# Weight groups narrowed in stages: one stage a step, with VectorE's background passes put ahead of the next step's own

## The chip, the cores and the metric

One core of one Trainium2 chip runs one program. The metric is device time in microseconds (us) for one execution; the kernel before takes 1035.78 us (median of 3 runs, 1034.14 to 1037.46). Engine names in the rows: PE is TensorE's matmul, PEld its weight load, DVE is VectorE, ACT is ScalarE, POOL is GpSimd, SP issues the DMAs.

## The reference, cut to what matters

```
X = np.fft.fft(np.fft.fft(x, axis=1), axis=2).real      # x: (2, 3008, 256)
t = X.reshape(6016, 256)
h = t @ w_in;  g = max(h, 0)**2;  t = g @ w_out          # w_in (256, 2048), w_out (2048, 256)
h = t @ w2_in; g = h / (1 + exp(-1.702 h)); return g @ w2_out
```

All values are float32. TensorE multiplies in the format `F32R`, so the kernel splits each operand into a high part (a cast to F32R) and a low part (the value less its high part) and sums three products: high times high, high times low, low times high.

## The kernel before, in words

The spectrum is folded by symmetry into 8 blocks of 378 or 376 columns, each in an even and an odd half. The first MLP is a list of 128 **steps**, `steps`; step i takes one block j and one slice f of 128 of the 2048 hidden features. In a step:

- TensorE runs `front1` (L442 to L456): six matmuls into a fresh PSUM tile `psa`, of which there are two. Front i+2 therefore waits until VectorE has read the tile of front i to its end.
- VectorE makes `p` (L710) and the two halves of `h` (L712, L713); the last of them frees the `psa` tile.
- ScalarE makes the squared ReLU (L719, L720) and the high part `gh` (L722). In twelve steps (the set `SV`) VectorE does the ReLU (L717) instead.
- GpSimd, or VectorE in the steps of `VSTEPS`, makes the low part `gl` (L76) of the step before.
- TensorE runs `back` (twelve matmuls, L468) for step i-4 (`LAG`), so an undisturbed step is 18 matmuls.

Where a run of steps on one block ends (after steps 3, 7, 15, 23, 35, 39, 47, 63, 79, 95, 111), `store` (L573 to L582) copies the two accumulators `psb` out four steps later, one on ScalarE, one on VectorE. The next block's `back` needs those PSUM tiles.

Beside the steps runs **background** work (L558), as generators: each item that a generator yields is one or a few instructions. The table `PLAN` gives each job a first step, a rate (items a step) and a step by which it must be done. From step 18 on (`THROTTLE`) a background instruction may not be issued ahead of the step's last `h` and `gh` (`issue_after`); otherwise a list scheduler orders each engine's queue, and VectorE's background passes may stand behind or in between the `p` and `h` of later steps. Every engine works its queue in the order in which it was written.

The job that the change touches most prepares a **group** of weights. The weights come as 64-bit words and are narrowed to float32 by `narrow` (L162 to L180): ScalarE takes an absolute value (L169), VectorE makes four passes (clamp L170, shift and mask L171, or-in of the sign L178, add L180), and the low word is scaled (L175 on ScalarE for the groups in `RA`, L177 on VectorE for the others). Then `widen` or `widen_in` makes high and low parts; for `widen_in` (the second MLP's first matrix) GpSimd makes four differences (L233) and the low parts `w2i` in two rounds, and for `widen` it makes the low part `w` in most groups. All groups of the second MLP go through one buffer `ue`, so ScalarE's and VectorE's first passes on a group wait until GpSimd has read the group before. The jobs are `conv` (six groups, steps 3 to 36), `w2a` (three groups, 55 to 78) and `w2b` (five groups, 85 to 117). Seven of the eight groups of `w2a` and `w2b` are not in `RA`.

`odd_k` (L398) makes the two odd blocks of a batch: `split_eo` casts them to a high and a low part `eo`, and `nyquist` has TensorE read both parts (L418, L419).

After the 128 steps the second MLP runs from a schedule written by hand; nothing of it is touched.

Of the kernel before, what the change touches and what calls it, by code (L numbers as in the profile page):

```python
# [13 lines left out]
ALU = mybir.AluOpType  # L14
# [49 lines left out]
def spectral_two_mlps_kernel(  # L64
# [7 lines left out]
    def f32(ap):  # L72
        return ap.bitcast(F32)
# [88 lines left out]
    def narrow(raw, ue, key=None):  # L162

        r = raw.rearrange("p (n w) -> p n w", w=2)
        lw, hw = r[:, :, 0], r[:, :, 1]
        u = ue[:, 0]
        uu, eu = u.bitcast(U32), ue[:, 1].bitcast(U32)

        yield lambda: A.activation(out=u, in_=f32(hw), func=AF.Abs)  # L169
        yield lambda: V.tensor_scalar(out=u, in0=u, scalar1=LEAST, scalar2=TOP, op0=ALU.max, op1=ALU.min)  # L170
        yield lambda: V.tensor_scalar(out=uu, in0=uu, scalar1=3, scalar2=0x3FFFFFF8,  # L171
                                      op0=ALU.logical_shift_left, op1=ALU.bitwise_and)

        if key in RA:
            yield lambda: A.activation(out=eu, in_=lw, func=AF.Copy, scale=2.0 ** -29)  # L175
        else:
            yield lambda: V.tensor_scalar(out=eu, in0=lw, scalar1=2.0 ** -29, scalar2=None, op0=ALU.mult)  # L177
        yield lambda: V.scalar_tensor_tensor(out=eu, in0=hw, scalar=0xC0000000, in1=eu,  # L178
                                             op0=ALU.bitwise_and, op1=ALU.bitwise_or)
        yield lambda: V.tensor_tensor(out=uu, in0=uu, in1=eu, op=ALU.add)  # L180
# [6 lines left out]
    def widen(mlp, kind, g, temps, dest, then=None, tag="xt"):  # L187
        low = G if LOW[mlp, kind, g] == "G" else V
        raw = raws.pop((mlp, kind, g))
        ue = temp(temps, tag)  # L190
        yield from narrow(raw, ue, (mlp, kind, g))
        if then:
            then()
        w = dest.tile([P, 2, 1024], F32R, tag="w", name="w")
        o = ue[:, 0]
        if (mlp, kind) == (0, 0):

            o = ue[:, 1]
            a, c = ue[:, 0, 0:512], ue[:, 0, 512:1024]
            yield lambda: (G if g in EOG else V).tensor_tensor(out=o[:, 0:512], in0=a, in1=c, op=ALU.add)  # L200
            yield lambda: V.scalar_tensor_tensor(out=o[:, 512:1024], in0=a, scalar=mask, in1=c,
                                                 op0=ALU.mult, op1=ALU.subtract)
        yield lambda: A.copy(w[:, 0], o)
        yield lambda: sub(low, w[:, 1], o, w[:, 0])
        if mlp and (kind, g) in PARKED:
            park((mlp, kind, g), w)
        weights[mlp, kind, g] = w

    parked = {}

# [187 lines left out]
    def odd_k(b, pool, tag="xt", later=0):  # L398

        wd = WID[2]  # L400
        w = temp(pool, tag).rearrange("p a b -> p (a b)")
        a = w[:, 0:wd]
        e2, e3 = (w[:, i * wd:(i + 2) * wd].rearrange("p (r k) -> p r k", r=2) for i in (1, 3))
        c0, c1 = cst[b, 2][:, :, 0:wd], cst[b, 3][:, :, 0:wd]

        def sums(par):
            pe = ps_a()
            z = (zc[b], zs[b])[par]
            halves(pe[:, 0, 0:wd], pe[:, 1, 0:wd],
                   [(z[:, :, 2 + par, 0:P], c0), (z[:, :, 3 - par, 0:P], c1)])  # L410
# [12 lines left out]

        yield lambda: sums(0)
        yield lambda: sums(1)
        yield lambda: split_eo(b, 2, e2)
        yield lambda: nyquist(2)
        while at_step[0] < later:
            yield lambda: None
        yield lambda: split_eo(b, 3, e3)  # L430
        yield lambda: nyquist(3)


# [94 lines left out]
    def at(name, job):  # L528
        i, rate, end = PLAN[name]
        plan.setdefault(i, []).append((name, rate, job))  # L530
        if end is not None:
# [3 lines left out]
    at("even01", lambda: even_k(0, 1, h_temps))  # L535
    at("odd0", lambda: odd_k(0, xp, "x2", 36))
    at("conv", lambda: chain(*(
        widen(0, k, g, xp, (winp, wq)[k], tag=("t", "x0")[k],
              then=(lambda k=k, g=g: load_w(0, k, g + 1)) if g < 3 else None)
        for g in (1, 2, 3) for k in range(2))))  # L540
    at("x3", lambda: iter([lambda: load_x(3)]))
    at("x4", lambda: iter([lambda: load_x(4)]))
# [99 lines left out]
    def w2_jobs(lo, hi):  # L642
        for i in range(lo, hi):
            k, g = order[i]
            dest = w2a if i < 6 else w2b
            then = (lambda i=i: load_w(1, *order[i + 2])) if i + 2 < 8 else (lambda: load_y(0)) if i == 6 else None
            if k == 0:
                yield from widen_in(g, temp(cv2), dest, then=then)
            else:
                yield from widen(1, 1, g, cv2, dest, then=then)  # L650

    def y_first():
        yB["odd"] = raw_tile(1, F32R).rearrange("p (a b) -> p a b", a=2)
# [26 lines left out]
        yield from y_job(j)  # L680

    held = []
    by_hand = ExitStack()
    for i in range(n):

        if i == PLAN["fold5"][2]:
# [17 lines left out]
        elif done:  # L704
# [2 lines left out]
        h = m.tile([P, 2, NP], F32, tag="h", name="h", bufs=4)  # L707
        hv = h[:, :, 0:wd]
        p = m.tile([P, NP], F32, tag="p", name="p")
        V.scalar_tensor_tensor(out=p[:, 0:wd], in0=e128[blocks[j]][:, 0:wd], scalar=w1n_t[:, 0, f:f + 1],  # L710
                               in1=ps[:, 0, 0:wd], op0=ALU.mult, op1=ALU.add)
        V.tensor_tensor(out=h[:, 0, 0:wd], in0=p[:, 0:wd], in1=ps[:, 1, 0:wd], op=ALU.add)  # L712
        last_v = V.tensor_tensor(out=h[:, 1, 0:wd], in0=p[:, 0:wd], in1=ps[:, 1, 0:wd], op=ALU.subtract)  # L713
        if done and done[3]:
            store(*done[:2])
        if i in SV:
            V.scalar_tensor_tensor(out=hv, in0=hv, scalar=0.0, in1=hv, op0=ALU.max, op1=ALU.mult)  # L717
        else:
            A.activation(out=hv, in_=hv, func=AF.Relu)  # L719
            A.activation(out=hv, in_=hv, func=AF.Square)  # L720
# [9 lines left out]
        if pend:  # L730
            low_part(*pend)
        pend = (i, (j, f), h, gh)
        with ExitStack() as behind:
            if THROTTLE <= i < n:
                behind.enter_context(tc.issue_after(last_v.ins))
                behind.enter_context(tc.issue_after(last_a.ins))
            background(i)
    low_part(*pend)
    assert not live
    fetch((1, 1, 2), winp)  # L740
# [258 lines left out]
```

## Time and profile before

| What | Value |
|---|---|
| median of 3 runs | 1035.78 us |
| the profiled execution | 1034.19 us, span 1032.1 us |
| PE busy | 987.3 us (96%) |
| DVE busy, ACT busy, POOL busy | 823.0, 616.4, 351.0 us |
| DVE copy of a store (L581), mean | 934 ns |
| POOL low part `gl` (L76), mean | 1913 ns |
| shorter gaps of PE ahead of a front (L453) at 277 and 449 us | 0.56, 0.38 us |
| gaps of PE ahead of L468 at 119.6 us and L453 at 124.8 us (step 20) | 0.47, 0.35 us |
| DVE, five passes of a group, instructions | L170 x16, L171 x16, L177 x8, L178 x16, L180 x16 at 128x1024 or 2048 |

The profiled execution's own time lies 2.1 us above its span and 1.6 us below the median. The profile counts an engine as busy from start to end of its instructions; PE's ends are modelled, so what counts there are the gaps: "idle before" an instruction, with the engine and line that ended it. Core and span are the only ones there are. The 128 steps lie between about 32 and 520 us.

### The profile page before, as it was taken

To read this page: it belongs to the slowest core of one execution; us is meant where nothing else is said; L and a number is where in the kernel's file an instruction comes from. 1 tells how busy PE (TensorE), PEld (TensorE's weight loads), DVE (VectorE), ACT (ScalarE), POOL (GpSimd) and SP (SyncE) were. 2 spreads that over 40 slices of the span, in tenths; PEclk is the share of its full clock that TensorE was granted. 3 is DMA by queue.
4 is the path that set the end of the run, shared out by engine and by line. 5 is a ranking of instruction groups with operands and counts; after the bars stand their busy time and mean duration, and the time that the engine had idled before them with its cause. 6 is when DMAs were issued, how large, how long until landed. Compare 5 with 4: busy or idle time off the path is not lost.

```text
span 1032.1 us, 14239 instructions
## 1 busy us (share of the span) xinstructions
PE 987.3 (96%) x5582; PEld 951.4 (92%) x5582; DVE 823.0 (80%) x1089; ACT 616.4 (60%) x764; POOL 351.0 (34%) x216
## 2 busy tenths in 40 slices
PE   8988988999989999898989999999999999999998
PEld 8578987898989799898989999999999999999997
DVE  7997889885877579677668888888988888888875
ACT  2576576775688578787754554554555455454443
POOL 2457474534567546776715210102020020200000
PEclk9898999999999999999999999999999999999999
DMA  7532212101142112101342100000100000000000
GB/s 286 209 108 80 72 71 82 72 31 53 42 140 85 72 67 88 70 32 61 114 138 94 61 31 30 30 32 7 54 1 30 31 31 31 1 31 1 31 1 30
DMA packets 22914, 65.22 MB, mean 63 GB/s; under 512 B 1856, under 2 KB 14272, under 8 KB 19648
## 3 DMA queue, kind: packets, MB, share of 16 engines
q1 hardware_dynamic: 22848, 64.32, 17.5%
q8 instruction: 43, 0.70, 0.3%
q14 instruction: 23, 0.19, 0.1%
HBM read 43.13 MB, written 21.19 MB: 62 GB/s over the span
## 4 chain that ended last, share of the span: by engine, by line
PE 53%; DVE 3%; ACT 2%; issue 1%; POOL 0%; DVEq 0%; ACTq 0%
PE psb L779 25%; PE psc L763 22%; PE psb L468 4%; ACT h L720 1%; ACT h L719 1%; PE psa L453 1%; PE psa L455 0%; PE psa L454 0%; DVE ue L177 0%; DVE gl L76 0%; DVE ue L178 0%; DVE ue L170 0%; ACT gh L722 0%; DVE yc L76 0%; DVE h L712 0%
## 5 line engine op out<-in xcount | busy, mean ns | idle before, releaser
L76 POOL TENSOR_TENSOR gl<-h,gh 128x752 fp32r<-128x752 f32 (+1 forms) x113 | 215.3, 1913 | 170.8 <-ACT gh L722 153.3
L468 PE MATMUL psb<-gh,w 128*128 128x376 f32 (+1 forms) x1024 | 244.4, 341 | 4.0 <-ACT o L581 3.4
L779 PE MATMUL psb<-gh,w 128*128 128x376 f32 (+1 forms) x1024 | 237.7, 334 | 0.0
L468 PEld LDWEIGHTS psb<-gh,w 128*128 128x128 f32 x1024 | 187.2, 193 | 5.5 <-ACT o L581 4.5
L779 PEld LDWEIGHTS psb<-gh,w 128*128 128x128 f32 x1024 | 182.9, 188 | 0.0
L719 ACT ACTIVATE h<-h 128x752 f32<-128x752 f32 (+1 forms) x116 | 96.5, 832 | 79.5 <-DVE h L713 77.3
L844 ACT ACTIVATE g<-c 128x1128 f32<-128x1128 f32 (+1 forms) x64 | 73.8, 1152 | 99.7 <-DVE c L842 99.7
L468 PE MATMUL psb<-gl,w 128*128 128x376 f32 (+1 forms) x512 | 133.1, 341 | 0.0
L779 PE MATMUL psb<-gl,w 128*128 128x376 f32 (+1 forms) x512 | 129.9, 335 | 0.4 <-DVE gl L76 0.3
L722 ACT CAST gh<-h 128x752 fp32r<-128x752 f32 (+1 forms) x128 | 105.3, 822 | 22.7 <-DVE h L717 19.5
L453 PE MATMUL psa<-eo,w 128*128 128x376 f32 (+1 forms) x256 | 90.3, 354 | 25.1 <-DVE h L713 15.1
L76 DVE TENSOR_TENSOR gl<-g,gh 128x1504 fp32r<-128x1504 f32 (+1 forms) x64 | 111.7, 1745 | 1.6 <-ACT gh L824 1.6
L824 ACT CAST gh<-g 128x1504 fp32r<-128x1504 f32 (+1 forms) x64 | 93.1, 1454 | 31.8 <-DVE g L815 31.8
L710 DVE SCALAR_TENSOR_TENSOR p<-n,w1n_t,psa 128x376 f32<-128x376 f32 (+1 forms) x128 | 75.9, 599 | 45.0 <-PE psa L455 44.9
L615 POOL TENSOR_TENSOR ue<-raw 128x376 f32<-128x376 f32 (+1 forms) x16 | 19.5, 1237 | 270.6 <-DVE ya L76 270.5
L720 ACT ACTIVATE h<-h 128x752 f32<-128x752 f32 (+1 forms) x116 | 96.7, 835 | 3.3
L468 PEld LDWEIGHTS psb<-gl,w 128*128 128x128 f32 x512 | 95.5, 194 | 0.0
L779 PEld LDWEIGHTS psb<-gl,w 128*128 128x128 f32 x512 | 92.1, 188 | 1.0 <-DVE gl L76 1.0
L815 DVE TENSOR_TENSOR g<-g,c 128x1128 f32<-128x1128 f32 (+1 forms) x64 | 89.5, 1399 | 1.2 <-ACT g L844 1.2
L841 DVE TENSOR_TENSOR g<-g,psc 128x376 f32<-128x376 f32 (+1 forms) x64 | 35.0, 546 | 68.9 <-ACT g L840 68.9
L454 PE MATMUL psa<-eo,w 128*128 128x376 f32 (+1 forms) x256 | 86.2, 337 | 0.0
L455 PE MATMUL psa<-eo,w 128*128 128x376 f32 (+1 forms) x256 | 86.1, 337 | 0.0
(138 smaller groups left out, 1627.8 us busy)
## 6 DMA issues: line engine op xcount, KB each, us to landing
ydram<-o SPq DMA_DIRECT2D x18, 376.0 KB, 2.8
xt<-in_x SPq DMA_DIRECT2D x5, 1024.0 KB, 7.0
cst<-in_dfts SPq DMA_DIRECT2D x8, 570.0 KB, 6.0
raw<-ydram SPq DMA_DIRECT2D x6, 752.0 KB, 4.6
out<-o SPq DMA_DIRECT2D x11, 376.0 KB, 3.1
raw<-in_w1i SPq DMA_DIRECT2D x4, 1024.0 KB, 5.8
raw<-in_w1o SPq DMA_DIRECT2D x4, 1024.0 KB, 7.3
raw<-in_w2i SPq DMA_DIRECT2D x4, 1024.0 KB, 4.9
```

What stands on the lines that cost most here:

```text
L76: eng.tensor_tensor(out=o, in0=a, in1=f32(b), op=ALU.subtract)
L453: T.matmul(o, lhsT=w[:, 0, fs], rhs=t[:, par, 0, 0:wd], start=True, stop=False)
L454: T.matmul(o, lhsT=w[:, 0, fs], rhs=t[:, par, 1, 0:wd], start=False, stop=False)
L455: T.matmul(o, lhsT=w[:, 1, fs], rhs=t[:, par, 0, 0:wd], start=False, stop=True)
L468: T.matmul(acc[j][ec][:, s, 0:wd], lhsT=w[:, hl, e0:e0 + P], rhs=(gh, gl)[gi][:, s, 0:wd], start=(first and hl == 0 and gi == 0), stop=(la ...
L719: A.activation(out=hv, in_=hv, func=AF.Relu)
L720: A.activation(out=hv, in_=hv, func=AF.Square)
L722: last_a = A.copy(gh[:, :, 0:wd], hv)
L763: T.matmul(bank, lhsT=w[:, hl, slot * P:(slot + 1) * P], rhs=t[:, yl, i], start=(first and hl == 0 and yl == 0), stop=(hl == 1), skip_grou ...
L779: T.matmul(o[:, s, 0:wd], lhsT=w[:, hl, e0:e0 + P], rhs=g[:, 2 * i + s, 0:wd], start=(f == 0 and hl == 0 and g is gh), stop=(f == 15 and h ...
L815: V.tensor_tensor(out=g[:, 1:4, 0:pw], in0=g[:, 1:4, 0:pw], in1=c[:, :, 0:pw], op=ALU.mult)
L824: A.copy(gh[:, :, 0:pw], g[:, :, 0:pw])
```

## The change

Four things. (1) `staged` wraps the weight jobs: the passes of a group are issued in packets, one packet a step, and the first packet (ScalarE's absolute value, with the scaling where that is ScalarE's) is kept in a list `early` and issued in the next step by `flush`, after the store's copies and ahead of the step's own ReLU; the scaling moves up behind the absolute value for `RA` groups. The rates fall to one packet a step or a little more. (2) `w2_jobs` adds an empty step behind a group whose low part is GpSimd's. (3) In the second batch, `nyquist` comes one step later behind `split_eo`. (4) The first `p` of a step may not stand ahead of VectorE's background instructions of the step before (`beside`).

```
-    "out0": (0, 12, 3), "even01": (0, 1, 4), "odd0": (1, 1, 48), "conv": (3, 2, 36),
+    "out0": (0, 12, 3), "even01": (0, 1, 4), "odd0": (1, 1, 48), "conv": (3, 1.2, 36),
-    "cst3": (66, 4, 67), "odd1": (79, 1, 88), "w2a": (55, 1.6, 78), "w2b": (85, 1.7, 117), "y0": (117, 1, 128),
+    "cst3": (66, 4, 67), "odd1": (79, 1, 88), "w2a": (55, 1, 78), "w2b": (85, 1.04, 117), "y0": (117, 1, 128),
...
         yield lambda: A.activation(out=u, in_=f32(hw), func=AF.Abs)
+        early = key in RA and key != (0, 0, 0)
+        if early:
+            yield lambda: A.activation(out=eu, in_=lw, func=AF.Copy, scale=2.0 ** -29)
...
+        if early:
+            pass
+        elif key in RA:
...
+    early = []
+
+    def flush():
+        while early:
+            early.pop(0)()
+
+    def staged(key, gen):
+
+        mlp, kind, _ = key
+        first = (2, 2, 2) if key in RA else (1, 3, 2)
+        yield lambda: early.append(lambda: run(gen, first[0]))
+        yield lambda: (flush(), run(gen, first[1]))
+        for k in first[2:] + ((1,) if kind else (4, 1, 2) if mlp else (2, 1)):
+            yield lambda: run(gen, k)
+        yield lambda: run(gen)
...
         yield lambda: split_eo(b, 2, e2)
+        yield from [lambda: None] * b
         yield lambda: nyquist(2)
...
         yield lambda: split_eo(b, 3, e3)
+        yield from [lambda: None] * b
         yield lambda: nyquist(3)
...
-                yield from widen_in(g, temp(cv2), dest, then=then)
+                yield from staged((1, 0, g), widen_in(g, temp(cv2), dest, then=then))
             else:
-                yield from widen(1, 1, g, cv2, dest, then=then)
+                yield from staged((1, 1, g), widen(1, 1, g, cv2, dest, then=then))
+            if LOW[1, k, g] == "G" and i < hi - 1:
+                yield lambda: None
...
+        for ins in beside:
+            tc.add_manual_dep(first_v.ins, ins.name,
+                              mybir.DependencyInfo(mybir.DependencyClass.NoSync, mybir.DependencyReason.DATA), reason="beside")
...
         if done and done[3]:
             store(*done[:2])
+        flush()
...
+        beside = [ins for ins in traced[mark:] if ins.engine == last_v.ins.engine] if THROTTLE <= i else []
```

VectorE's queue from step 56 to 59, where the first group of `w2a` is narrowed (`ue` is the group's buffer, `raw` its words). Before:

```order
L170 TENSOR_SCALAR ue<-ue 128x1024
L710 SCALAR_TENSOR_TENSOR p<-n,w1n_t,psa 128x376
L171 TENSOR_SCALAR ue<-ue 128x1024
L712 TENSOR_TENSOR h<-p,psa 128x376
L713 TENSOR_TENSOR h<-p,psa 128x376
L177 TENSOR_SCALAR ue<-raw 128x1024
L710 SCALAR_TENSOR_TENSOR p<-n,w1n_t,psa 128x376
L712 TENSOR_TENSOR h<-p,psa 128x376
L713 TENSOR_TENSOR h<-p,psa 128x376
L178 SCALAR_TENSOR_TENSOR ue<-raw,ue 128x1024
L710 SCALAR_TENSOR_TENSOR p<-n,w1n_t,psa 128x376
L180 ISA ue<-ue 128x2048
```

and now (the same passes have the lines L173, L182, L174, L183, L185; `p` is L735, `h` L740 and L741):

```order
L173 TENSOR_SCALAR ue<-ue 128x1024
L182 TENSOR_SCALAR ue<-raw 128x1024
L174 TENSOR_SCALAR ue<-ue 128x1024
L735 SCALAR_TENSOR_TENSOR p<-n,w1n_t,psa 128x376
L740 TENSOR_TENSOR h<-p,psa 128x376
L741 TENSOR_TENSOR h<-p,psa 128x376
L183 SCALAR_TENSOR_TENSOR ue<-raw,ue 128x1024
L185 ISA ue<-ue 128x2048
L735 SCALAR_TENSOR_TENSOR p<-n,w1n_t,psa 128x376 x2
L740 TENSOR_TENSOR h<-p,psa 128x376
L741 TENSOR_TENSOR h<-p,psa 128x376
```

The five passes stood one by one between the `p` and `h` of four steps; now three stand together ahead of one step's `p`, and two ahead of the next one's.

VectorE's queue from step 99 to 101, where the group (1, 1, 0) is narrowed and a block is stored (`o` is the store's copy). Before:

```order
L177 TENSOR_SCALAR ue<-raw 128x1024
L170 TENSOR_SCALAR ue<-ue 128x1024
L581 COPY o<-psb 128x2x376
L171 TENSOR_SCALAR ue<-ue 128x1024
L710 SCALAR_TENSOR_TENSOR p<-n,w1n_t,psa 128x376 x2
L712 TENSOR_TENSOR h<-p,psa 128x376
L713 TENSOR_TENSOR h<-p,psa 128x376
L178 SCALAR_TENSOR_TENSOR ue<-raw,ue 128x1024
L712 TENSOR_TENSOR h<-p,psa 128x376
L713 TENSOR_TENSOR h<-p,psa 128x376
```

and now:

```order
L182 TENSOR_SCALAR ue<-raw 128x1024
L183 SCALAR_TENSOR_TENSOR ue<-raw,ue 128x1024
L604 COPY o<-psb 128x2x376
L173 TENSOR_SCALAR ue<-ue 128x1024
L174 TENSOR_SCALAR ue<-ue 128x1024
L185 ISA ue<-ue 128x2048
L735 SCALAR_TENSOR_TENSOR p<-n,w1n_t,psa 128x376 x2
L740 TENSOR_TENSOR h<-p,psa 128x376
L741 TENSOR_TENSOR h<-p,psa 128x376
L740 TENSOR_TENSOR h<-p,psa 128x376
L741 TENSOR_TENSOR h<-p,psa 128x376
```

At this place the rate of 1.04 puts two packets into one step: all five passes and the copy now stand ahead of the two `p`, and the copy comes behind two passes instead of two others.

GpSimd's queue from step 93 to 102, where it makes the low parts `w2i` of the group in front of that one (`gl` is the steps' own low part). Before:

```order
L76 TENSOR_TENSOR gl<-h,gh 128x2x376 x3
L76 TENSOR_TENSOR w2i<-ue,w2i 128x512
L76 TENSOR_TENSOR w2i<-ue,w2i 128x384
L76 TENSOR_TENSOR gl<-h,gh 128x2x376 x2
L76 TENSOR_TENSOR w2i<-ue,w2i 128x512
L76 TENSOR_TENSOR w2i<-ue,w2i 128x384
L76 TENSOR_TENSOR gl<-h,gh 128x2x376 x4
L76 TENSOR_TENSOR w<-ue,w 128x1024
```

and now:

```order
L76 TENSOR_TENSOR gl<-h,gh 128x2x376 x2
L76 TENSOR_TENSOR w2i<-ue,w2i 128x512
L76 TENSOR_TENSOR w2i<-ue,w2i 128x384
L76 TENSOR_TENSOR gl<-h,gh 128x2x376
L76 TENSOR_TENSOR w2i<-ue,w2i 128x512
L76 TENSOR_TENSOR w2i<-ue,w2i 128x384
L76 TENSOR_TENSOR gl<-h,gh 128x2x376 x5
L76 TENSOR_TENSOR w<-ue,w 128x1024
```

The last `w2i` stood behind five of the `gl` shown and now stands behind three, with five steps' `gl` to come before the next weight instruction.

On TensorE the two `sel_t` matmuls of `nyquist` (L418, L419) stood between the matmuls of the front next to them; now they stand behind the `back` that follows, ahead of the next front.

## Rows read from the trace of the kernel before

**Rows 1.** Timeline: an undisturbed step, then passes in a queue. Start, duration, instruction.
```profile
432.35 0.33 PE L453 MATMUL psa<-eo,w 128*128 128x376 f32 x1
...
434.23 0.54 DVE L713 TENSOR_TENSOR h<-p,psa 128x376 f32<-128x376 f32 x1
...
435.45 0.33 PE L453 MATMUL psa<-eo,w 128*128 128x376 f32 x1
```
**Rows 2.** Waits of PE, 85 to 95 us: line, releaser, total us, times, longest.
```profile
PE psa L453 <- DVE h L713: 2.3, 2, 2.0
```
**Rows 3.** Waits of PE, 130 to 160 us.
```profile
PE psa L453 <- DVE h L713: 2.8, 3, 1.4
PE psa L453 <- DVE p L710: 1.4, 1, 1.4
```
**Rows 4.** Waits of PE, 300 to 325 us.
```profile
PE psa L453 <- DVE p L710: 3.7, 2, 2.7
PE psa L453 <- DVE h L713: 0.7, 2, 0.3
```
**Rows 5.** Waits of PE, 330 to 385 us.
```profile
PE psa L419 <- POOL eo L76: 1.9, 1, 1.9
```
**Rows 6.** Waits of PE, 420 to 426 us.
```profile
PE psb L468 <- ACT o L581: 2.6, 1, 2.6
PE psb L468 <- DVE o L581: 0.6, 1, 0.6
```
**Rows 7.** Timeline of PE, 470 to 481 us: the fronts that waited.
```profile
472.61 0.44 PE L453 MATMUL psa<-eo,w 128*128 128x376 f32 x1 [1.77 <-DVE h L713]
...
477.90 0.44 PE L453 MATMUL psa<-eo,w 128*128 128x376 f32 x1 [1.41 <-DVE p L710]
...
479.39 0.68 PE L453 MATMUL psa<-eo,w 128*128 128x376 f32 x1 [0.72 <-DVE h L713]
```
**Rows 8.** Windows: stretch, length, busy PE, PEld, DVE, ACT, POOL, granted clock, DMA, GB/s.
```profile
90.20:96.80 6.60, 6.25 (x19) 5.75 (x20) 5.13 (x8) 6.28 (x8) 3.70 (x3) 0.50 0.33 119
144.20:148.10 3.90, 3.90 (x15) 3.90 (x15) 3.03 (x6) 2.77 (x4) 1.80 (x2) 0.56 0.01 4
362.70:366.40 3.70, 3.70 (x13) 3.70 (x14) 1.85 (x3) 1.20 (x3) 0.00 (x0) 0.54 0.00 0
424.60:427.90 3.30, 3.30 (x11) 3.30 (x12) 3.30 (x6) 1.21 (x2) 1.80 (x1) 0.51 0.33 119
479.40:482.60 3.20, 3.20 (x11) 3.20 (x12) 3.06 (x6) 2.98 (x5) 3.20 (x3) 0.52 0.64 231
```
**Rows 9.** Timeline of DVE: two weight passes with their idle time and releaser.
```profile
295.95 1.14 DVE L170 TENSOR_SCALAR ue<-ue 128x1024 f32<-128x1024 f32 x1 [4.27 <-ACT ue L169]
...
420.82 2.25 DVE L177 TENSOR_SCALAR ue<-raw 128x1024 uint32<-128x1024 uint32 x1 [3.57 <-POOL w2i L76]
```
**Rows 10.** Waits of ACT, 410 to 425 us.
```profile
ACT ue L169 <- POOL w2i L76: 3.1, 1, 3.1
```
**Rows 11.** Groups by form on DVE: count, busy us, mean ns, idle before.
```profile
L180 DVE CUSTOM_DVE_ANT_0 ue<-ue 128x2048 uint16<-128x2048 uint16 x16 | 25.4, 1588 | 0.0
L178 DVE SCALAR_TENSOR_TENSOR ue<-raw,ue 128x1024 uint32<-128x1024 uint32 x16 | 24.3, 1517 | 1.4 <-ACT ue L175 1.3
L170 DVE TENSOR_SCALAR ue<-ue 128x1024 f32<-128x1024 f32 x16 | 21.4, 1336 | 6.8 <-ACT ue L169 6.6
L171 DVE TENSOR_SCALAR ue<-ue 128x1024 uint32<-128x1024 uint32 x16 | 15.8, 986 | 0.1
L177 DVE TENSOR_SCALAR ue<-raw 128x1024 uint32<-128x1024 uint32 x8 | 14.5, 1813 | 6.1 <-POOL w2i L76 4.8 <-POOL w L76 1.2
```
**Rows 12.** Timeline of DVE: two steps' p in a row, then the pass behind them.
```profile
425.05 1.11 DVE L710 SCALAR_TENSOR_TENSOR p<-n,w1n_t,psa 128x376 f32<-128x376 f32 x2
...
426.99 1.21 DVE L178 SCALAR_TENSOR_TENSOR ue<-raw,ue 128x1024 uint32<-128x1024 uint32 x1
```
**Rows 13.** Timeline of DVE: the last two passes of the group at 264 us.
```profile
270.48 2.60 DVE L178 SCALAR_TENSOR_TENSOR ue<-raw,ue 128x1024 uint32<-128x1024 uint32 x1
...
273.52 2.75 DVE L180 CUSTOM_DVE_ANT_0 ue<-ue 128x2048 uint16<-128x2048 uint16 x1
```
**Rows 14.** Timeline of DVE: the low part of the last split ahead of the second MLP.
```profile
511.10 1.99 DVE L76 TENSOR_TENSOR ya<-ue,ya 128x756 fp32r<-128x756 f32 x1 [1.55 <-ACT ya L622]
```

More of the change, by code (lines that the diff above doesn't have):

```diff
@@ L172, in narrow @@
                                       op0=ALU.logical_shift_left, op1=ALU.bitwise_and)
-        if key in RA:
+        if early:
+            pass
+        elif key in RA:
             yield lambda: A.activation(out=eu, in_=lw, func=AF.Copy, scale=2.0 ** -29)
@@ L537, in spectral_two_mlps_kernel @@
     at("conv", lambda: chain(*(
-        widen(0, k, g, xp, (winp, wq)[k], tag=("t", "x0")[k],
-              then=(lambda k=k, g=g: load_w(0, k, g + 1)) if g < 3 else None)
+        staged((0, k, g), widen(0, k, g, xp, (winp, wq)[k], tag=("t", "x0")[k],
+                                then=(lambda k=k, g=g: load_w(0, k, g + 1)) if g < 3 else None))
         for g in (1, 2, 3) for k in range(2))))
@@ L682, in spectral_two_mlps_kernel @@
     held = []
-    by_hand = ExitStack()
+    beside = []
     for i in range(n):
@@ L709, in spectral_two_mlps_kernel @@
         p = m.tile([P, NP], F32, tag="p", name="p")
-        V.scalar_tensor_tensor(out=p[:, 0:wd], in0=e128[blocks[j]][:, 0:wd], scalar=w1n_t[:, 0, f:f + 1],
-                               in1=ps[:, 0, 0:wd], op0=ALU.mult, op1=ALU.add)
+        first_v = V.scalar_tensor_tensor(out=p[:, 0:wd], in0=e128[blocks[j]][:, 0:wd], scalar=w1n_t[:, 0, f:f + 1],
+                                         in1=ps[:, 0, 0:wd], op0=ALU.mult, op1=ALU.add)
+        for ins in beside:
+            tc.add_manual_dep(first_v.ins, ins.name,
+                              mybir.DependencyInfo(mybir.DependencyClass.NoSync, mybir.DependencyReason.DATA), reason="beside")
         V.tensor_tensor(out=h[:, 0, 0:wd], in0=p[:, 0:wd], in1=ps[:, 1, 0:wd], op=ALU.add)
@@ L732, in spectral_two_mlps_kernel @@
         pend = (i, (j, f), h, gh)
+        traced = nc.cur_bb.bb.instructions
+        mark = len(traced)
         with ExitStack() as behind:
```

## The prediction

> **What bounds the kernel now.** I read the page's busy shares first: TensorE is busy for 987 of 1032 us, so nothing that the change does to another engine counts unless it moves a gap of TensorE. Then I listed TensorE's waits by stretch. From the start of the second MLP on there are almost none, and the change touches nothing there. The gaps that matter lie between 56 and 516 us, among the first MLP's steps. The timeline shows the rhythm of an undisturbed step [rows 1]: from one front to the next TensorE takes 435.45 - 432.35 = 3.10 us, and VectorE's last `h` ends 434.23 + 0.54 - 432.35 = 2.42 us behind the front. The front two steps on needs that `h` and comes at 6.20, so VectorE may be 3.8 us late before TensorE stops. Where it is later, TensorE's front waits for `p` or `h`; that is what nearly all rows of TensorE's waits name.
>
> The reader is to see four kinds of such stops, all beside weight work.
>
> First, waits behind GpSimd. A weight pass on VectorE cannot start because GpSimd still reads the buffer `ue`, or because ScalarE's absolute value waits for the same thing; it stood idle for 4.27 and 3.57 us [rows 9], ScalarE for 3.1 [rows 10], and each engine works its queue in order, so the next `p`, `h` or store copy stood behind it. TensorE lost 3.7 + 0.7 [rows 4], 2.6 + 0.6 [rows 6] and 1.8 + 1.4 + 0.7 us [rows 7], together 11.5. Second, `nyquist` waited 1.9 us for GpSimd's low part, in the middle of a front [rows 5]. Third, two groups of the first MLP that followed each other closely: 2.8 + 1.4 us [rows 3]. Fourth, weight passes hoisted ahead of the `h` of a step before 18: 2.3 us [rows 2].
>
> Behind five of these stops the granted clock fell to about half, 1.2 instead of 2.4 GHz [rows 8]. At half clock a stretch does half its work, so its loss is its length times one less its clock: 6.6 x 0.50 = 3.3, 3.9 x 0.44 = 1.7, 3.7 x 0.46 = 1.7, 3.3 x 0.49 = 1.6 and 3.2 x 0.48 = 1.5 us.
>
> **The change part by part: what it takes away.** The empty step behind a GpSimd group puts the next group's first pass 3.1 us later, and GpSimd's last `w2i` stands two `gl` (1.9 us each, in the table) sooner in its queue: some 6.9 us of room, and the longest idle time that it has to cover is 4.27 [rows 9]. I take the waits behind GpSimd as gone: 11.5, and with them the two clock dips at 424 and 479, 3.1. Sum 14.6. If it covered nothing, this term would be zero; see the rivals.
>
> `nyquist` one step later: a step is 3.1 us and the wait was 1.9 [rows 5], so it goes, with its dip: 3.6. The odd block's `p` needs the result only steps later, so the delay itself is covered; without that cover it would cost one step, 3.1.
>
> The conv groups, at 1.2 packets a step instead of 2 passes, start their passes on different steps: the pair that collided at 130 to 160 is drawn apart. I take 4.2 and its dip of 1.7 as gone here, 5.9, and put what remains of it below. The pass that was hoisted ahead of step 10 now comes after step 18: 2.3 and its dip of 3.3, 5.6. Sum of all four: 14.6 + 3.6 + 5.9 + 5.6 = 29.7 us.
>
> **What it adds.** No pass is added or taken away; the five passes of a group are packed. Their mean durations are 1.34 (L170), 1.81 (L177), 0.99 (L171), then 1.52 (L178) and 1.59 (L180) [rows 11]: 4.1 in the first packet of a group outside `RA`, 3.1 in the second. In a queue, two `p` and two `h` take 426.99 - 425.05 = 1.94 us [rows 12], so one `p` with its two `h` takes about 1.5. Count from the front of the step in which the first packet is issued. VectorE's own work ends at 2.4; the first packet at 6.5; the next step's `h` at 8.0, and TensorE needs it at 9.3; the second packet at 11.1; two `p` and the two `h` at 13.1, and TensorE needs them at 12.4. So such a group stops TensorE for 0.7 us; a group in `RA` has no L177 and stops it for nothing. If L178 and L180 run at 1.21 us [rows 12] it is nothing too; if they run as at 264 us, 2.60 and 2.75 [rows 13], it is 2.9. Between these I take the mean. Of seven such groups, five stand alone: 3.5 us, less the 1.0 that groups at the same places cost now (the shorter stops in the table, 0.56 and 0.38), leaves 2.5.
>
> The other places are those where packets meet a store. Step 99: all five passes (7.3) and the copy (0.9) ahead of two `p`. From 2.4 the `h` of step 100 ends at 2.4 + 7.3 + 0.9 + 1.9 = 12.5. TensorE has two fronts and two backs to do in front of it after the next step begins (1.0 and 2.1 each, 6 and 12 of the 18 matmuls of 3.10 us): 3.1 + 2.0 + 4.2 = 9.3, and the copy comes late by about 0.9 of that, so the stop is 12.5 - 9.3 - 0.9 = 2.3 us (0 at the short pass durations, 4.5 at the long). Step 115: the group of step 113 (0.7) and the copy behind it (0.9 less what the gap between groups gives back): 1.4. Step 20: a whole second packet and the copy ahead of two `p`, by the same counting 2.3, less the 0.8 that stands there now (in the table): 1.5. Steps 27 to 31: passes, copy and three low parts on VectorE: 2.3. Steps 10 to 12: ScalarE's two weight passes now stand ahead of the store's copy: 1.5 with the front behind it. At each of these the ends are nothing and twice the value.
>
> `nyquist`'s cast in step 84 stands ahead of the next `p`: 0.9, between nothing and the 1.9 of the old wait. At step 124 `ya` stands ahead of a `p` that used to run in front of it; it held VectorE for 1.55 idle and 1.99 busy [rows 14]. This is the last work before the second MLP, whose start waits for ScalarE's and VectorE's last step, so a delay goes to the end: between 0 and 3.5, I take the middle, 1.9. The early packets on ScalarE delay the ReLU and `gh` by one pass; `back` comes four steps later (`LAG`), which hides it. Where that cover is gone, at a store, ScalarE's copy is late, and 2.6 us [rows 6] is what that cost once. The DMA loads of the weights follow the passes to other steps, and the next group's words arrive steps ahead of their use: nothing, and if a load were late, at most a packet's wait of one step, 3.1.
>
> A dip of the clock comes back where stops are long: five of some nine long stops have one now, four of the new places lie over 1.4, so I count two of 1.6: 3.2. Sum: 2.5 + 2.3 + 1.4 + 1.5 + 2.3 + 1.5 + 0.9 + 1.9 + 3.2 = 17.5 us.
>
> Net 29.7 - 17.5 = 12.2 us less. The profiled execution took 1034.2, so 1022.0; the median of the runs lies 1.6 above it, so **1023** to 1024 on that scale. I say 1023.
>
> **The rivals.** (a) The packets collide with GpSimd: **slower**. At 264 us L178 and L180 took 2.60 and 2.75 [rows 13] instead of 1.21 [rows 12], with GpSimd at work beside them. If the pairs of packed passes always met this, each second packet would be 2.2 longer: 9 places (five groups, four stores) x 2.2 = 20, with two more dips 23, against the 12.2: 1035.8 + 11 = 1047. For it: the packets stand back to back, with no `p` between in which GpSimd's instruction could end. Against it: the mean over all 16 groups is 1.5. It decides from 12.2 / 9 = 1.4 us more a place on, a pair of 4.5 instead of 3.1. The Trainium skill has the rule behind this: SBUF — State Buffer, section "SBUF: two separate sides", says that VectorE and GpSimd take a shared port pair as an exclusive lock for a whole instruction, and that the other one blocks. By that rule the two rows differ because one pass waited for a `gl`; the trace agrees in kind, and does not tell how often the new order will meet it.
>
> (b) The change doesn't do what it says: GpSimd is still late where the next group's pass comes, since it also makes the steps' `gl`, and the 14.6 us stay. Then +2.4: 1038, **no change**. For it: the wait is inherited from `gl`s that come late when the steps are late. Against it: the room given is longer than the longest wait seen.
>
> (c) The packets run at the short durations and the piles cost nothing: five groups, four stores and a dip less give back about 10 us: 1013. For it: 1.21 us is what L178 takes with nothing in its way [rows 12]. Against it: the means.
>
> **How the numbers follow.** My forecast, a gain of 5 to 22 us, has 0.57: 1014 to 1031. Rival (c) has 0.13, (a) 0.13, (b) and other ways to no change 0.14, and 0.03 lies between. Within 0.3% is 1032.7 to 1038.9, about what a measurement of this kernel can tell from no change. Faster: 0.57 + 0.13 + 0.03 and what of (a) ends just below, 0.74; same 0.14; slower 0.12. The range is 1009 to 1037: it takes in (c) and most of (b), and leaves out (a) and a little below.
>
> **What would show it.** Right, if in the profile after the weight passes no longer show idle time behind GpSimd, the `nyquist` wait on GpSimd is gone, VectorE's idle ahead of `p` falls in the steps of `w2a` and `w2b`, and the stops that remain lie at the stores (steps 20, 28, 100, 116) with 1 to 3 us each. TensorE's total gaps, 45 us now, should come to some 33. Wrong, if L178 and L180 have a mean well above 1.6; if the first pass of a group still waits for GpSimd or ScalarE; if the second MLP's start is more than 2 us later relative to the last front; or if the clock dips are as many as now.

## The result, and the profile after

The changed kernel is **slower by 0.8%**: 1042.38 us (median of 5 runs, 1041.42 to 1043.34) against 1035.67 (5 runs, 1033.23 to 1037.46), ratio 1.0079, interval 1.0061 to 1.0097. The forecast was 1023, and the range ended at 1037. The profiled execution took 1041.83 us, its span 1039.6.

First, TensorE's waits in the changed kernel (line, releaser, total us, times, longest): 110 to 187 us, then 330 to 385 (the old `nyquist` wait), then 385 to 500. `front1` is now L476 to L478, `back` L491, `p` L735, `h` L740 and L741, the copy of a store L604.

```profile
PE psb L491 <- POOL gl L76: 2.7, 2, 2.0
PE psb L491 <- DVE o L604: 2.3, 2, 1.6
PE psa L476 <- DVE p L735: 1.8, 3, 0.6
...
PE psa L476 <- DVE h L741: 0.7, 1, 0.7
PE psa L476 <- DVE p L735: 0.3, 2, 0.2
...
PE psa L476 <- DVE p L735: 4.7, 4, 2.5
PE psb L491 <- POOL gl L76: 3.6, 1, 3.6
PE psa L476 <- DVE h L741: 2.1, 5, 0.6
PE psb L491 <- DVE o L604: 2.0, 1, 2.0
```

The wait of [rows 5] is gone. But `back` now waits for GpSimd's `gl`, which cost nothing before. From 385 to 500 us the waits add up to 12.4 us. In the kernel before, the four entries of the same stretch, which [rows 6] and [rows 7] are part of, add up to 7.5:

```profile
PE psa L453 <- DVE h L713: 2.9, 3, 1.8
PE psb L468 <- ACT o L581: 2.6, 1, 2.6
PE psa L453 <- DVE p L710: 1.4, 1, 1.4
PE psb L468 <- DVE o L581: 0.6, 1, 0.6
```

The weight passes (count, busy us, mean ns, idle before), to be held against [rows 11]:

```profile
L185 DVE CUSTOM_DVE_ANT_0 ue<-ue 128x2048 uint16<-128x2048 uint16 x16 | 27.8, 1736 | 0.3
L183 DVE SCALAR_TENSOR_TENSOR ue<-raw,ue 128x1024 uint32<-128x1024 uint32 x16 | 24.6, 1538 | 0.0
L173 DVE TENSOR_SCALAR ue<-ue 128x1024 f32<-128x1024 f32 x16 | 18.2, 1140 | 4.0 <-ACT ue L169 4.0
L182 DVE TENSOR_SCALAR ue<-raw 128x1024 uint32<-128x1024 uint32 x8 | 16.0, 2000 | 0.3 <-POOL w2i L76 0.3
```

VectorE's passes wait for GpSimd almost no longer (0.3 us, 6.1 before), and the second packet's pair is 3.27 us against 3.1. By these signs the change did what it should. But TensorE's gaps, forecast to fall from 45 us to some 33, are 1039.6 less 991.8 busy, 47.8. Part of the loss stands elsewhere on VectorE, in background work that the prediction passed over: a pass heads the queue, idle until ScalarE is done, and `p` stands behind it. The timeline of VectorE at four places (start, duration, idle before):

```profile
366.09 1.99 DVE L76 TENSOR_TENSOR eo<-ue,eo 128x752 fp32r<-128x752 f32 x1 [3.35 <-ACT eo L383]
...
385.15 2.06 DVE L76 TENSOR_TENSOR w<-ue,w 128x1024 fp32r<-128x1024 f32 x1 [3.29 <-ACT w L208]
387.13 0.59 DVE L735 SCALAR_TENSOR_TENSOR p<-n,w1n_t,psa 128x376 f32<-128x376 f32 x1
...
461.32 7.58 DVE L182 TENSOR_SCALAR ue<-raw 128x1024 uint32<-128x1024 uint32 x1
...
514.68 1.98 DVE L76 TENSOR_TENSOR ya<-ue,ya 128x756 fp32r<-128x756 f32 x1 [3.40 <-ACT ya L645]
```

The three idle places (366, 385 and 515 us) show the kind more than the size: TensorE's waits right behind them are 0.2, 1.3 and 0.6 us. The pass at 461.32, which took 7.58 us, is of another kind. GpSimd at that time, and 30 us later; then its first add of the y work in the kernel before, which waited for nothing:

```profile
461.18 7.17 POOL L76 TENSOR_TENSOR gl<-h,gh 128x752 fp32r<-128x752 f32 x4
...
489.12 3.41 POOL L628 TENSOR_TENSOR raw<-raw,ue 128x1512 f32<-128x1512 f32 x1 [2.71 <-DMA ue<-ydram]
...
487.32 3.46 POOL L605 TENSOR_TENSOR raw<-raw,ue 128x1512 f32<-128x1512 f32 x1
```

Four `gl` run without a gap from 461.18 to 468.35, and the pass ends 0.55 us behind the last. At 489 the first add of the y work waits for its load, runs 3.41 us, and two `gl` stand behind it. TensorE at both places:

```profile
470.80 0.44 PE L476 MATMUL psa<-eo,w 128*128 128x376 f32 x1 [2.46 <-DVE p L735]
...
494.31 0.68 PE L491 MATMUL psb<-gl,w 128*128 128x376 f32 x1 [3.59 <-POOL gl L76]
```

The windows around three stops show the granted clock (the figure behind the five engines):

```profile
417.00:428.00 11.00, 8.21 (x34) 7.26 (x35) 10.93 (x12) 4.16 (x6) 6.22 (x3) 0.84 0.52 165
470.00:480.00 10.00, 8.51 (x37) 7.74 (x38) 9.70 (x16) 5.85 (x8) 0.00 (x0) 0.83 0.09 33
492.00:502.00 10.00, 7.68 (x30) 7.69 (x31) 2.61 (x5) 3.66 (x6) 10.00 (x9) 0.66 0.00 0
```

Where the time goes shows best when the same step is laid beside itself. VectorE's last `h` ends each step's claim on `psa`. At step 99 it ends at 417.25 us before and 414.05 after (start and duration of the row), so the changed kernel is 3.2 us ahead; at step 127 it is 4.8 behind. The rows of step 99, before and after, then of step 127:

```profile
416.71 0.54 DVE L713 TENSOR_TENSOR h<-p,psa 128x376 f32<-128x376 f32 x1
...
413.51 0.54 DVE L741 TENSOR_TENSOR h<-p,psa 128x376 f32<-128x376 f32 x1
...
515.85 0.54 DVE L713 TENSOR_TENSOR h<-p,psa 128x376 f32<-128x376 f32 x1
...
520.64 0.54 DVE L741 TENSOR_TENSOR h<-p,psa 128x376 f32<-128x376 f32 x1
```

The same for the runs below, each less the kernel before, us (one execution each; where a program is the same up to a step, as e14 and before up to step 55, they differ by up to 3):

| step | after | e2 no rule | e5 rule on packets | e6 rule on rest | e13 conv packets | e14 second MLP's packets | e15 conv, empty steps |
|---|---|---|---|---|---|---|---|
| 17 | -5.6 | -5.0 | -4.2 | -6.0 | -4.3 | -2.7 | -5.4 |
| 33 | -6.7 | -10.9 | -6.8 | -10.8 | -10.1 | -2.7 | -11.3 |
| 51 | -1.8 | -11.4 | -7.6 | -5.9 | -9.7 | -2.7 | -11.2 |
| 81 | -3.2 | -13.1 | -10.2 | -8.6 | -9.8 | -6.2 | -12.0 |
| 99 | -3.2 | -16.2 | -12.4 | -9.9 | -12.8 | -9.4 | -15.1 |
| 118 | -2.5 | -16.9 | -10.7 | -11.3 | -14.4 | -8.8 | -19.6 |
| 127 | +4.8 | -13.4 | -4.5 | -7.0 | -12.7 | -5.3 | -14.1 |
| end of the span | +7.5 | -12.0 | -3.9 | -3.6 | -10.7 | -3.1 | -15.9 |

The last row differs from the one above it by up to 3.4 us, although nothing of the second MLP was touched: what differs is its start, where TensorE waits for VectorE's `u` (2.8 us before, 3.8 after).

### The profile page after: what moved, and what is told of

Its sections match the earlier page's. It is cut to its first block, busy times and chain, and to the rows that moved or that the text cites. A ratio compares the mean times of both kernels' runs of the same rounds, so it can differ in the third digit from the quotient of the medians.

```text
span 1039.6 us, 14243 instructions
## 1 busy us (share of the span) xinstructions
PE 991.8 (95%) x5582; PEld 948.5 (91%) x5582; DVE 825.9 (79%) x1089; ACT 609.9 (59%) x764; POOL 355.5 (34%) x216
## 4 chain that ended last, share of the span: by engine, by line
PE 52%; DVE 7%; issue 2%; ACT 2%; POOL 1%; DVEq 0%; POOLq 0%; ACTq 0%
PE psb L811 24%; PE psc L795 22%; PE psb L491 4%; DVE ue L182 1%; POOL gl L76 1%; DVE p L735 1%; PE psa L476 1%; DVE h L741 1%; DVE ue L185 1%; DVE gl L76 1%; PE psa L478 1%; PE psa L477 1%; DVE ue L174 1%; ACT h L748 1%; ACT h L749 0%
## 5 line engine op out<-in xcount | busy, mean ns | idle before, releaser
L76 POOL TENSOR_TENSOR gl<-h,gh 128x752 fp32r<-128x752 f32 (+1 forms) x113 | 219.2, 1951 | 176.6 <-ACT gh L751 138.0
L491 PE MATMUL psb<-gh,w 128*128 128x376 f32 (+1 forms) x1024 | 243.2, 340 | 7.5 <-DVE o L604 5.1
L491 PEld LDWEIGHTS psb<-gh,w 128*128 128x128 f32 x1024 | 185.4, 192 | 10.6 <-DVE o L604 6.3
L491 PE MATMUL psb<-gl,w 128*128 128x376 f32 (+1 forms) x512 | 133.3, 341 | 6.3 <-POOL gl L76 6.3
L476 PE MATMUL psa<-eo,w 128*128 128x376 f32 (+1 forms) x256 | 91.5, 359 | 20.0 <-DVE p L735 10.0
L735 DVE SCALAR_TENSOR_TENSOR p<-n,w1n_t,psa 128x376 f32<-128x376 f32 (+1 forms) x128 | 75.6, 600 | 33.4 <-PE psa L478 33.3
L491 PEld LDWEIGHTS psb<-gl,w 128*128 128x128 f32 x512 | 94.4, 193 | 7.2 <-POOL gl L76 7.2
L740 DVE TENSOR_TENSOR h<-p,psa 128x376 f32<-128x376 f32 (+1 forms) x128 | 69.7, 545 | 22.6 <-POOL gl L76 11.6
L477 PE MATMUL psa<-eo,w 128*128 128x376 f32 (+1 forms) x256 | 86.1, 337 | 0.0
```

The lines of the kernel that those rows point to most:

```text
L76: eng.tensor_tensor(out=o, in0=a, in1=f32(b), op=ALU.subtract)
L476: T.matmul(o, lhsT=w[:, 0, fs], rhs=t[:, par, 0, 0:wd], start=True, stop=False)
L477: T.matmul(o, lhsT=w[:, 0, fs], rhs=t[:, par, 1, 0:wd], start=False, stop=False)
L491: T.matmul(acc[j][ec][:, s, 0:wd], lhsT=w[:, hl, e0:e0 + P], rhs=(gh, gl)[gi][:, s, 0:wd], start=(first and hl == 0 and gi == 0), stop=(la ...
L735: first_v = V.scalar_tensor_tensor(out=p[:, 0:wd], in0=e128[blocks[j]][:, 0:wd], scalar=w1n_t[:, 0, f:f + 1], in1=ps[:, 0, 0:wd], op0=ALU. ...
```

## The experiments

Each run was timed beside the kernel before; "to before" is its median less that of the kernel before, and the changed kernel has +6.7 on that scale. "The rule" is the fourth edit, `beside`. Three theories were held against each other: A, the rule costs, since VectorE stands idle with `p` queued; B, the packets collide with GpSimd; C, the slower groups make the y work on GpSimd late.

| run | us | to before | ratio, interval |
|---|---|---|---|
| e1 the rule alone | 1067.46 | +32.7 | 1.0307, 1.0281 to 1.0333 |
| e2 changed, no rule | 1021.20 | -13.5 | 0.9871, 0.9846 to 0.9895 |
| e3 `nyquist` delay alone | 1032.23 | -2.5 | 0.9971, 0.9955 to 0.9988 |
| e4 changed, single packets | 1038.02 | +3.3 | 1.0028, 1.0013 to 1.0043 |
| e5 changed, rule on packets alone | 1030.34 | -4.9 | 0.9961, 0.9944 to 0.9978 |
| e6 changed, rule on the rest alone | 1031.39 | -3.9 | 0.9969, 0.9959 to 0.9978 |
| e7 changed, three `gl` on VectorE | 1040.32 | +5.1 | 1.0056, 1.0039 to 1.0072 |
| e8 changed, y add behind `gl` | 1037.70 | +2.5 | 1.0027, 1.0016 to 1.0038 |
| e9 e2 with single packets | 1023.57 | -12.0 | 0.9886, 0.9868 to 0.9904 |
| e10 e2 without empty steps | 1020.88 | -14.7 | 0.9855, 0.9839 to 0.9870 |
| e11 e2 without `early` | 1022.60 | -13.0 | 0.9869, 0.9851 to 0.9887 |
| e12 e2, single packets, two empty steps | 1021.66 | -13.9 | 0.9862, 0.9844 to 0.9880 |
| e13 `nyquist` and conv packets | 1022.45 | -12.2 | 0.9882, 0.9862 to 0.9902 |
| e14 `nyquist` and second MLP's packets | 1031.61 | -3.1 | 0.9969, 0.9955 to 0.9984 |
| e15 e13 and empty steps, old rates | 1018.16 | -16.5 | 0.9845, 0.9827 to 0.9862 |

**e1, the rule alone**, put into the kernel before:

```
+        for ins in beside:
+            tc.add_manual_dep(first_v.ins, ins.name, ...)
```

> The kernel before, with only the rule that the first p of a step stands behind VectorE's background work of the step before; no packets, old rates, no delay of nyquist. Theory A (the order rule is what costs: in the changed kernel VectorE stood idle 3.3 us ahead of an eo at 366, 3.3 ahead of a w at 385 and 3.4 ahead of a ya at 515 us, each time for ScalarE and with p queued behind it): slower than before by 4 to 9 us, 1040 to 1045. Theory B (the packets collide with GpSimd's runs of gl, and the order rule does nothing by itself): 1034 to 1038. Theory C (the slower w2b makes the y work on GpSimd late, a stop of 3.6 us at 494 us): also 1034 to 1038, without that stop.

It was worse than any theory had it. VectorE's waits (total us, times, longest) and the longest of them:

```profile
DVE ue L170 <- ACT ue L169: 49.3, 8, 9.1
...
447.74 1.10 DVE L170 TENSOR_SCALAR ue<-ue 128x1024 f32<-128x1024 f32 x1 [9.09 <-ACT ue L169]
```

In eight places VectorE stood still for ScalarE's absolute value with `p` behind the waiting pass; before, the scheduler let `p` go first, and the same waits came to 6.6 us [rows 11]. In the changed kernel they are 4.0 us: the early packets serve the rule.

**e2, the changed kernel without the rule** (those lines left out):

> The changed kernel without the order rule; packets, rates, empty steps and the delay of nyquist stay. Theory A: the 4 to 9 us come back, 1033 to 1038. Theory B: the pass of 7.6 us at 461 us and the slow packet at 414 to 425 us stay, 1040 to 1044. Theory C: the 3.6 us stop of back on gl at 494 us stays and the time falls by less than 2, 1040 to 1043.

Theory A holds, and by more than it said: 20.2 us come back. Neither the pass of 7.6 us nor the stop at 494 us is left. What is left is in ScalarE's waits from 390 to 460 us and in TensorE's from 385 to 480:

```profile
ACT ue L169 <- POOL w2i L76: 9.7, 2, 5.2
...
PE psb L491 <- ACT o L604: 4.0, 1, 4.0
PE psb L491 <- POOL gl L76: 2.2, 2, 1.3
PE psb L491 <- ACT gh L748: 1.7, 1, 1.7
PE psa L476 <- DVE h L738: 0.3, 1, 0.3
```

TensorE's 8.2 us here are no less than before (7.5 in the four entries above). ScalarE's absolute value waits for `w2i`, and the store's copy, the ReLU and `gh` stand behind it.

**e3, the delay of `nyquist` alone**:

```
+        yield from [lambda: None] * b
         yield lambda: nyquist(2)
```

> The kernel before, with only nyquist one step later in the second batch. If the stop of 1.9 us and its clock dip of 1.7 are a term of their own: 1032 to 1033, 2.5 to 3.6 less than before. If VectorE is no earlier by it and the next stop takes what is won: 1035 to 1036, the same.

A term of its own, 2.5 us.

**e4, single packets**: the last five groups start a step earlier and never get two packets in one step.

```
-"w2b": (85, 1.04, 117)
+"w2b": (84, 1, 117)
```

> The changed kernel with the last five groups started one step earlier at exactly one packet a step, so that no step gets two packets. If the two packets of step 99 are the cost there (stops of 2.0, 0.4 and 0.3 us at 420 to 427 us and a dip of the clock of some 1.5): 1038 to 1040, 2.5 to 4 us less than the changed kernel. Theory B (each packet that meets a run of gl is slow, wherever it stands): no gain, 1040 to 1044, the slow passes only in other places. Theory C: the y work starts one step earlier and the stop at 494 us shrinks, up to 3.6 less again, 1035.

3.4 us less than the changed kernel, the size expected; the edit also moves all five groups by a step. The stop behind `gl` stayed at 3.6 us, which speaks against the part on theory C; the pass of 7.6 us was 2.3 here.

**e5 and e6, the rule divided**: in e5 it holds for the five narrowing passes alone, in e6 for all other background work of VectorE.

```
-        for ins in beside:
+        names = {q.ins.name for q in passes}
+        for ins in [x for x in beside if x.name in names]:      # e5; "not in" for e6
```

> The changed kernel with the order rule for the narrowing passes of the weights alone; every other background instruction of VectorE (eo, w, the folds, yb, ya) may stand behind p again. Theory A1 (the rule costs because VectorE waits idle for ScalarE ahead of eo, w and ya with p behind it): close to the kernel without the rule, 1021 to 1027. Theory A2 (it costs because whole packets of 3 to 4 us stand ahead of p, as the terms added in the prediction have it): most of the loss stays, 1033 to 1042.

> The complement: the order rule for all background instructions of VectorE but the narrowing passes. Theory A1: most of the loss stays, 1034 to 1042. Theory A2: 1021 to 1028. If both this and the run with the rule on the passes alone lie in between, the loss is shared.

Neither theory by itself. Against e2 the packets cost 8.6 us and the rest 9.6, and their sum of 18.2 is nearly the 20.2 of the whole rule. The table by steps says where: the packets lose 4.1 by step 33 (the conv groups), the rest nothing there but 5.5 between steps 33 and 51, where the folds of the input and the last `eo` of the first batch are made. TensorE's waits from 187 to 260 us, in the changed kernel, then in e2:

```profile
PE psa L476 <- DVE p L735: 2.3, 3, 1.5
PE psa L476 <- DVE h L741: 2.3, 3, 1.5
...
PE psa L476 <- DVE p L735: 0.3, 1, 0.3
```

**e7, `gl` of steps 110 to 112 on VectorE** in the changed kernel:

```
-VSTEPS = {..., 89, 113}
+VSTEPS = {..., 89, 110, 111, 112, 113}
```

> The changed kernel with the low parts of steps 110, 111 and 112 made on VectorE instead of GpSimd. If the pass of 7.6 us at 461 us (L182) was held up by the four gl that GpSimd ran one behind the other beside it: that pass takes 0.7 to 2.4 us, TensorE's stop of 2.5 us at 470 us shrinks to under 1, VectorE gets 3 gl of 0.93 us more, and the time falls by 1 to 3.5 us, to 1039 to 1041. If the pass is slow for another reason: it stays over 5 us and the time rises to 1043 to 1045.

The pass that took 7.58 us:

```profile
465.71 0.68 DVE L182 TENSOR_SCALAR ue<-raw 128x1024 uint32<-128x1024 uint32 x1
```

With nothing on GpSimd beside it, the same pass takes 0.68 us. So GpSimd's run of `gl` held it up. With the three `gl` added to VectorE counted in, the edit won 1.6 us.

**e8, the y add behind `gl`** in the changed kernel:

```
+                if j == 0:
+                    tc.add_manual_dep(r.ins, lows[-1].ins.name, ...)
```

> The changed kernel with GpSimd's first add of the y work (raw) put behind the gl that was written ahead of it; in the changed kernel it stood three gl further up, waited 2.7 us for its DMA and ran 3.4 us, and back waited 3.6 us for a gl behind it. No other engine's order changes. Theory C: that stop is gone, and the time falls by 2 to 5 us (the stop and a dip of the clock), 1037 to 1040. If the y work is late by it and the second MLP starts later by as much: 1041 to 1043.

4.2 us less, with no change on any other engine's queue. TensorE's waits from 480 to 524 us are now 0.6 us in all, and the second MLP starts no later for it:

```profile
PE psa L476 <- DVE h L747: 0.4, 1, 0.4
PE psb L491 <- POOL gl L76: 0.2, 1, 0.2
```

**e9 to e12, variants without the rule**: e9 has the edit of e4, e10 leaves out the empty step, e11 replaces `early.append(...)` and `flush()` by a plain `run(gen, first[0])`, e12 is e9 with two empty steps behind the two groups of `w2b` that make `w2i`.

> The changed kernel without the order rule and with single packets from step 84 on, the two edits that each gave a gain. If they add: the single packets gave 4.4 under the rule, 1021.2 less 4.4 = 1017. If the two packets of step 99 cost only because the rule put them ahead of p: 1020 to 1022, no gain over the kernel without the rule; the stop of 4.0 us at 408 us behind ScalarE's copy, whose absolute value waits 4.5 us for w2i, stays.

> The changed kernel without the order rule and without the empty step behind GpSimd's groups. If the empty steps are what took the waits behind GpSimd away (14.6 us in the prediction): ScalarE's and VectorE's first passes wait some 3 us longer for w2i in each group and the time rises by 4 to 12 us over the kernel without the rule, 1025 to 1033. If the packets alone did it: 1020 to 1023.

> The changed kernel without the order rule and without the list early: the first packet (ScalarE's absolute value) is issued with the background work, behind the step's ReLU and gh. If the early packet costs where it waits for w2i (4.5 and 5.2 us idle on ScalarE at 401 and 448 us, with the store's copy, the ReLU and gh behind it, stops of 4.0 and 3.0 us on TensorE): 1014 to 1018. If the early packet pays for itself by starting VectorE's passes sooner: 1022 to 1026.

> The changed kernel without the order rule, with single packets from step 84 on and two empty steps instead of one behind the second MLP's groups whose w2i GpSimd makes. If the waits of ScalarE's absolute value for w2i (4.5 and 5.2 us) are what is left: 1012 to 1017, with those waits under 2 us. If the later groups make the y work late: 1018 to 1024, with a stop behind gl at some 490 us or a later start of the second MLP.

All four lie between 1020.9 and 1023.6. The two packets of step 99 cost only under the rule. The empty steps brought nothing here, one or two, against what I expected: ScalarE's waits for `w2i` were 9.4 us with none (and 3.1 for a `w`), 9.7 with one and 8.7 with two (e12). Without `early` (e11) those waits are gone, and the time stays: from 385 to 480 us TensorE then waits 9.1 us in all, for `h`, `p`, `gl` and the store's copy.

**e13 to e15, the gain divided.** e13 is the kernel before with the delay of `nyquist` and `staged` for `conv` (rate 1.2); e14 has `staged`, rates and empty steps in the second MLP's groups instead; e15 is e13 with the empty steps alone:

```
+            if LOW[1, k, g] == "G" and i < hi - 1:
+                yield lambda: None
```

> The kernel before with the nyquist delay and the packets of the conv groups (rate 1.2); the groups of the second MLP as before, without empty steps, no order rule. If the conv terms of the prediction hold (5.6 for the hoisted pass and 5.9 for the pair, less 1.5 to 4 for what is added there) beside the 2.5 to 3 of nyquist: 1020 to 1024. If most of the gain is from the second MLP's groups: 1028 to 1032.

> The kernel before with the nyquist delay, the packets, rates and empty steps of the second MLP's groups; the conv groups as before at rate 2, no order rule. If the waits behind GpSimd go (14.6 us in the prediction): 1018 to 1024. If they only move to other places (4.0 and 3.0 us at 408 and 451 us in the kernel without the rule): 1029 to 1033, little beside the 2.5 to 3 us of nyquist.

> As the run with the packets of the conv groups alone, and the empty step behind GpSimd's groups at the old rates (1.6 and 1.7 items a step). If the empty step by itself takes the waits behind GpSimd away (idle 4.3 and 3.6 us ahead of two passes of VectorE): 5 to 14 us less than the conv packets alone. If not: within 2 us of it.

Beside `nyquist`, the conv packets give 9.7 us and the second MLP's packets 0.6, which is not clear of noise. In e14 ScalarE waits as in e2; below it, TensorE's waits of e14 from 385 to 505 us:

```profile
ACT ue L169 <- POOL w2i L76: 9.6, 2, 5.1
...
PE psb L491 <- ACT o L604: 4.0, 1, 4.0
PE psb L491 <- POOL gl L76: 3.2, 3, 1.3
PE psb L491 <- ACT gh L748: 1.7, 1, 1.7
```

At the old rates the empty step gives 4.3 us more, and e15, with the ratio 0.9845, is the fastest version found. It is not by ScalarE's wait for `w2i`, which is 3.0 us in e13 and 5.2 in e15. In the profiled executions both reach the second MLP at the same time, 502.8 and 502.9 us; there e15 waits 1.4 us for `u` where e13 waits 3.7, and in the 20 us from there its clock is 1.00 instead of 0.91. The two make 2.3 + 1.8 = 4.1. Why the second MLP starts better in e15 was not tested. The wait for `w2i` in e13 and e15, then the wait for `u` in both:

```profile
ACT ue L169 <- POOL w2i L76: 3.0, 1, 3.0
...
ACT ue L169 <- POOL w2i L76: 5.2, 2, 3.0
...
PE psc L790 <- DVE u L846: 3.7, 1, 3.7
...
PE psc L792 <- DVE u L848: 1.4, 1, 1.4
```

## Why the prediction failed

**The step that failed most** is "I take the waits behind GpSimd as gone: 11.5, and with them the two clock dips at 424 and 479, 3.1." Of these 14.6 us, 0.6 came (e14 less e3). The part at [rows 4] did come. The run e3, which the table by steps leaves out, stands at -1.8, -1.5, -4.5 and -4.5 at steps 51, 81, 99 and 127, so e14 is better than e3 by 0.9, 4.7, 4.9 and 0.8: some 4 us are won by step 81 and lost again by step 127. At the places of [rows 6] and [rows 7], other stops stand in place of the old ones: 4.0 us behind ScalarE's copy, 1.7 behind `gh` and 3.2 behind `gl`. VectorE's passes did stop waiting for GpSimd, as said. But a packet begins with ScalarE's absolute value, which waits for the same `w2i`, and `early` put it ahead of the ReLU, `gh` and the next store's copy: 9.7 us of waits on ScalarE in e2, with stops of 4.0 and 1.7 us on TensorE. I had costed this at nothing, hidden by `LAG`, though [rows 10] showed the wait. `early` decides where the stop stands, not that there is one: e11 leaves it out and takes no less time. What would remove the stop stays open. At one packet a step `w2i` is also made over more steps, which may be why the room of "some 6.9 us" was not there; that was not measured by itself. Rival (b) had said that GpSimd would still be late.

One part of the 11.5 was also misread. Ahead of the stops of [rows 7], VectorE waited only 1.24 us for GpSimd; then three passes ran slowly beside GpSimd's `gl`:

```profile
464.63 2.29 DVE L177 TENSOR_SCALAR ue<-raw 128x1024 uint32<-128x1024 uint32 x1 [1.24 <-POOL w2i L76]
466.85 2.30 DVE L170 TENSOR_SCALAR ue<-ue 128x1024 f32<-128x1024 f32 x1
...
469.59 2.06 DVE L171 TENSOR_SCALAR ue<-ue 128x1024 uint32<-128x1024 uint32 x1
```

At 0.68 us each, which is what they take in e7 with GpSimd idle, they would have ended 4.6 us sooner. The room that an empty step gives was reckoned for a wait, not for this; it is rival (a)'s mechanism, at work in the kernel before.

**The second failed step** is what the rule costs outside the weight groups. I priced two places, 0.9 for the `eo` of step 84 and 1.9 for `ya`, 2.8 in all. The rule binds every background pass of VectorE, and the rest cost 9.6 (e6), 5.5 of it at folds and `eo` in steps 33 to 51, a stretch that the prediction does not mention. I read the rule off the two places that I looked at. What `ya` cost at the end, forecast at 1.9, can't be told from the rest: from the last `h` to the end it is 518.4 us in the changed kernel, 517.1 in e2 without the rule and 515.7 before.

**Terms that held.** The conv groups: 5.6 + 5.9 less 1.5 for steps 10 to 12 is 10.0; measured 9.7. `nyquist`: 3.6; measured 2.5. The rule on the packets: 2.5 + 2.3 + 1.4 + 1.5 + 2.3 is 10.0; measured 8.6, but that is luck in part. By the table, e5 less e2, 4.1 fall to the conv groups by step 33 (forecast 3.8), only 2.1 between steps 33 and 118 (forecast 6.2), and 2.7 behind step 118, where the prediction has no packet and TensorE waits 3.6 us for `gl` behind the y add. Step 99's double packet: 2.3 and part of a dip; measured 3.4 (e4). Only the dips were sized too small, two of 1.6: the three windows above lose 1.8 + 1.7 + 3.4 = 6.9 by the length times one less the clock.

With the measured sizes the sum comes out: -12.2, and 14.0 for GpSimd, 1.1 for `nyquist`, 0.3 for conv, 6.8 for the rest of the rule, 2.0 for what both halves of the rule cost together, less 1.4 for the packets and less the 3.2 of dips that the measured terms contain, is +7.4. Measured is +6.7. The rule's 20.2 is itself the changed kernel less e2, so what this sum tests is that the gains of e3, e13 and e14 add up to 12.8 where e2, which has them all, gains 13.5.

**Rival (a)** (packets collide with GpSimd) named a real mechanism and the wrong weight. It struck hardest once, at 461 us, for 1.6 us by e7, while the mean pair of second passes rose by 0.17 us only. The Trainium skill, SBUF — State Buffer, section "SBUF: two separate sides", has the shared port pair as an exclusive lock for whole instructions; the trace agrees, and shows more than the page states: the pass at 461 us did not get in between four `gl`, but waited for all of them. That is not how it always goes: at 414.31 us the same pass met four `gl` in a row too, and took 2.28 us, about one `gl` and its own length. What decides between the two was not tested.

**Not foreseen at all**: GpSimd's order changed too. The kernel before has two `gl` between the low part `w` and the first add of the y work, the changed kernel one; so the add stands there before its load has come, and it cost 4.2 us (e8). The second MLP's packets brought this and not the rule: e2 and e14 have the same order, and e1, with the rule alone, has the old one. Without the rule it costs less: TensorE's longest stop behind `gl` at that place in e2 is 1.0 us. I had not looked at the end of the program on this engine.

## What to carry to other kernels

An order rule on an in-order engine is paid at every instruction that it binds, not at those it was written for: list them all, and for each ask which other engine it waits for and what now stands behind it. When a wait is taken from one engine, look for the instruction that starts the same work on the next engine; if it waits for the same buffer, the stop moves with it. Of four edits made together, one cost 20 us and hid 13.5 that the others gave, so undo them one at a time before judging any.

## What the hardware showed that I had not expected

One VectorE pass of 128x1024 words took 0.68 us with GpSimd idle, 7.58 us beside four GpSimd instructions in a row, and 2.28 us beside another four, while `p` and `h`, which read PSUM, kept their 0.60 and 0.55 us beside GpSimd (459.66 and 460.40 us in the changed kernel, beside `w2i`).
